# A written order for the first phases of an attention and expert kernel, with its scales taken another way

## The chip, the core and the metric

The kernel runs on one core of a Trainium2 chip. The core has a matrix engine (PE), a vector engine (DVE), an activation engine (ACT), a general engine (POOL, GpSimd) and a queue that issues loads and stores (SP). Each takes its own instructions in order and waits for the others by semaphores. The metric is device microseconds (us) of one execution, lower is better. Profiled and timed executions are of the same program on the same inputs.

## The reference

```python
q, k, v: (8, 12, 448, 64) float32     # batch, heads, tokens, head size
w_in: (768, 2048) float64, w_out: (2048, 768) float64
scores = scale * q @ k.T - log(448)   # scale = 1 / sqrt(64)
attn   = 1 / (1 + exp(-scores))       # a sigmoid, not a softmax
x      = (attn @ v), heads side by side: (8 * 448, 768)
h      = x @ w_in
g      = where(h > 0, h, exp(min(h, 0)) - 1)
out    = g @ w_out                    # (3584, 768) float32
```

The weights arrive as float64. The kernel turns them into numbers that its engines can work on with integer instructions on the words.

## The kernel before

**Numbers in two parts.** Most matmuls work on float16 pairs: a float32 tile times a power of two gives a high part (ACT, line 139, a product rounded to float16) and a low part (DVE, line 140, the same product less the high part). A product of two such numbers takes three matmuls (high by high, low by high, high by low). The power of two comes from the greatest magnitude of the tile: a reduction, or a matmul with ones that sums magnitudes over the partitions, then a floor (`max`), the exponent's bits (`bitwise_and`, lines 103 to 107 and 179 to 186) and a reciprocal.

**Weights.** w_in is cut into 16 tiles of 128 columns (768 KB of float64 each), w_out into two halves of 16 tiles (384 KB each). `magnitudes` (line 150) builds a float32 number from the words of a float64: two ACT passes (lines 156 and 160), a DVE pass (161), and a matmul with ones that sums the magnitudes. `signed` (172) puts the sign back with a second DVE pass. Then the tile is split in two (139 and 140). `w_in_tile` does all of it for w_in and leaves the result in `wi`; `load_w_out` is a generator that does it for w_out, one step at a time.

**Buffers.** `stage` (line 195) holds five float64 tiles of w_in and five float32 tiles. It carries the tag "wo", which is also that of `wo` (line 693), w_out's own tile; both lie in one buffer, one after the other. `g`, the hidden layer, has a tag that it shares with `early`, the float32 keys and queries of batch 0. PSUM has three buffers of tag "pm", two of "psc" and one of "pav".

**Stages.** For each of 8 batches there are 6 pairs of heads. Batch 0 (EXACT = 1) computes its attention in float32: `transposed` turns q and k on PE (line 362), `scores` (408), a sigmoid on ACT (416), `values` (480 and 468), `finish` (`xh`, high and low part and its greatest magnitude). From batch 1 on, q and k are split first ("nat", then a transposing DMA to "qk"), and from the ninth pair on the values too. When six pairs are done, `rescale` brings the six parts of `xh` to one scale (521), `greatest` finds its power of two, and `moe1` computes 16 tiles of the hidden layer: 18 matmuls each (570), an exponential (582), two DVE passes (584 and 585) and the split into `g`. `moe2` multiplies `g` by w_out (602) and writes the result (610 and 612).

**Order.** For the first part, up to batch 0's hidden layer, a planner with a time model orders the instructions of each engine. The loop there takes pair after pair of batch 0 with some tiles of w_in behind each (`W_IN`), and `w_out_beside` puts w_out's steps beside batch 0's hidden layer. From line 779 on, the order of PE, ACT, DVE and SP is that of the program text: the attention of batch b runs beside `moe2` of batch b - 1, whose steps `fill` hands out between scores and values. The rest of w_out's steps stand at the first pairs of batch 1 (`step`, line 825). `beside` prepares two pairs of the next batch during `moe1`. POOL is left to the planner throughout. Sigmoids of a batch are made to follow the last exponential of the batch before (`last_exp`), so that the activation tables change once each way.

**Scales.** `value_scale` keeps, pair after pair, the greatest value scale (`vm`) and its reciprocal (`vi`) on DVE. `moe_scales` makes the 16 factors of the exponential (`m[:, 0]`) and of the split (`m[:, 1]`) in three DVE instructions.

Of the kernel before, what the change touches and what calls it, by code (L numbers as in the profile page):

```python
# [32 lines left out]

@with_exitstack
def attention_ffn(
# [24 lines left out]
    WHOLE = EXACT * NP + 2  # L60
    SP = 4
    SKEW = 2
    W_IN = [1, 3, 6, 9, 12, 15, 16]
    W_LOAD = [1, 1]
    W_OUT = 4
    W_AHEAD = [6, 2]
# [12 lines left out]
    wi = const.tile([P, 2, NK, DF], F16, name="wi")  # L79


    wp = const.tile([P, NF], F32, name="wp")
    wr = const.tile([P, NF], F32, name="wr")
# [6 lines left out]
    stage, w_in_words = [], []  # L90
    ones = const.tile([P, P], BF16, name="ones")
    nc.vector.memset(ones, 1.0)
    half = const.tile([P, 2], BF16, name="half")
# [14 lines left out]

    def greatest(dst, mx):
# [4 lines left out]
        def rest():  # L114
            pb = ps.tile([P, 512], F32, tag="pm", name="pb", bufs=3)
            nc.tensor.matmul(pb[:, :P], ones, dg, start=True, stop=True)
            al = sb.tile([P, 1], F32, tag="al", name="al", bufs=2)
            nc.vector.tensor_reduce(al, pb[:, :P], axis=AX.X, op=ALU.max)
            power_of_two(dst, al, XTINY)

        return rest

    def sums_of_rows(dst, mx, parts):

        n = mx.shape[1]

        def rest():
            pb = ps.tile([P, 512], F32, tag="pm", name="pr", bufs=3)
            sums = pb[:, : 4 * n].rearrange("p (n x) -> p n x", x=4)
            for r in parts:  # L130
                nc.tensor.matmul(sums[r], ones[:, r], mx, start=True, stop=True)
            al = sb.tile([P, n], F32, tag="al", name="al", bufs=2)
            nc.vector.tensor_reduce(al, sums, axis=AX.X, op=ALU.max)
            power_of_two(dst, al, TINY)

        return rest

    def split(hi, lo, src, s):
        nc.scalar.mul(hi, src, s)  # L139
        nc.vector.scalar_tensor_tensor(lo, src, s, hi, op0=ALU.mult, op1=ALU.subtract)  # L140
# [9 lines left out]
    def magnitudes(t, lo, hi, hl, sums, start, stop):  # L150


        u, h = t.bitcast(U32), hi.bitcast(F32)


        nc.scalar.activation(t, h, AF.Abs, scale=2.0**-112)


        top = hl.bitcast(U16).rearrange("p a (c t) -> p a c t", t=4)[:, :, :, 1]
        nc.scalar.activation(lo, top, AF.Copy, scale=2.0**-13, bias=2.0**-14 - 0.5)  # L160
        nc.vector.scalar_tensor_tensor(
            u, u, 3, lo, op0=ALU.logical_shift_left, op1=ALU.bitwise_or
        )

        top = t.bitcast(BF16).rearrange("p a (c t) -> p a c t", t=2)[:, :, :, 1]
        n = t.shape[1]
        for c in range(n):
            nc.tensor.matmul(
                sums, ones, top[:, c], start=start and c == 0, stop=stop and c == n - 1
            )  # L170
# [17 lines left out]
    def load_w_in(n):  # L188

        src = w_in.rearrange("(c p) f -> p c f", p=P)  # L190
        for _ in range(n):
            f = len(w_in_words)
            if f == 0:

                stage.append(sb.tile([P, WR * 2 + WT, NK * P], F32, tag="wo", name="stage"))
            if f < NF:
                st = stage[0][:, f % WR * 2 : f % WR * 2 + 2]
                st = st.rearrange("p a c -> p (a c)").rearrange("p (c x) -> p c x", c=NK)
                nc.sync.dma_start(st.bitcast(U64), src[:, :, f * P : (f + 1) * P])
                w_in_words.append(words(st))  # L200

    def w_in_tile(f):
        lo, hi, hl = w_in_words[f]
        t = stage[0][:, WR * 2 + f % WT].rearrange("p (c x) -> p c x", c=NK)
        sums = ps.tile([P, 512], F32, tag="pm", name=f"si{f}", bufs=3)
        magnitudes(t, lo, hi, hl, sums[:, :P], True, True)
        sum_magnitude(wp[:, f : f + 1], sums[:, :P])
        nc.vector.reciprocal(wr[:, f : f + 1], wp[:, f : f + 1])
        s = sb.tile([P, 1], F32, tag="sw", name=f"swi{f}", bufs=2)
        nc.gpsimd.tensor_scalar(s, wr[:, f : f + 1], 2.0**WTOP, None, op0=ALU.mult)  # L210
        d = wi[:, :, :, f * P : (f + 1) * P]
        signed(t, hi)
        split(d[:, 0], d[:, 1], t, s)
# [6 lines left out]
    def load_w_out(wo):  # L220


        for i in range(NH):
            whole = [
                wo[:, i, f + SKEW].rearrange("p j c -> p (j c)").bitcast(F32)
                for f in range(NF - SKEW)
            ] + [
                sb.tile([P, HM], F32, tag="o", name=f"to{i}_{f}", bufs=OB) for f in range(SKEW)
            ]
            sums = ps.tile([P, 512], F32, tag="pav", name=f"so{i}")  # L230
            loads = []

            def load(f):
                if f >= NF:
                    return
                if i == 0 and f >= 2:
                    st = wo[:, 1, f % 8 * 2 :][:, :2]
# [12 lines left out]
                loads.append(st)  # L250

            early = W_AHEAD[i]
            for f in range(early):
                load(f)
            for f in range(NF):
                load(f + early)
                lo, hi, hl = words(loads[f])
                t = whole[f].unsqueeze(1)
                magnitudes(t, lo, hi, hl, sums[:, :HM], f == 0, f == NF - 1)
                signed(t, hi)  # L260
                yield
            sum_magnitude(wop[:, i : i + 1], sums[:, :HM])
# [3 lines left out]
            for f in range(NF):  # L266
                split(wo[:, i, f, 0], wo[:, i, f, 1], whole[f], s[:, 1 + f : 2 + f])
                yield


    last_exp = {}
# [3 lines left out]
    def load_qk(b, hp):  # L275
# [3 lines left out]
        for i, src in enumerate((q, k)):  # L279
            for j in range(2):  # L280
                nc.sync.dma_start(  # L281
                    raw[:, i * (NC + 1) :][:, :NC, j],
                    src[b, h0 + j, :SM].rearrange("(p c) d -> p c d", c=NC),
                )
# [19 lines left out]
    def value_scale(b, hp, pv, c, xs):  # L304
# [3 lines left out]
        if hp:  # L308
            nc.vector.tensor_tensor(vm[:, hp : hp + 1], vm[:, hp - 1 : hp], pv, op=ALU.max)
        else:  # L310
            nc.gpsimd.tensor_copy(vm[:, 0:1], pv)
        nc.vector.reciprocal(vi[:, hp : hp + 1], vm[:, hp : hp + 1])
        if b * NP + hp < WHOLE:
            nc.gpsimd.tensor_scalar(c, vi[:, hp : hp + 1], 2.0 ** (XTOP - XBITS), None, op0=ALU.mult)
        else:
            nc.gpsimd.tensor_scalar(
                c, vi[:, hp : hp + 1], pv, 2.0 ** (XTOP - XBITS - TOP - ATOP),
# [3 lines left out]
    def prepare(b, hp, raw, rv, xs):  # L321


        u = f"{b}_{hp}"
        n = 1 if b < EXACT else 3
        mx = sb.tile([P, 15], BF16, tag="mx", name=f"mx{u}", bufs=2)
        groups = mx.rearrange("p (n x) -> p n x", x=5)[:, :n, :4]
        absmax(mx[:, 0:4], rv.rearrange("p (a t) d -> p a (t d)", a=4))
        if n > 1:

            absmax(mx[:, 6 : 2 * NC + 7], raw.rearrange("p t h d -> p t (h d)"))
            nc.vector.tensor_tensor(
                mx[:, 5:14:8], mx[:, 9:10].to_broadcast([P, 2]), half, op=ALU.mult
            )
        pw = sb.tile([P, n], F32, tag="pw", name=f"pw{u}", bufs=2)
        apart = b >= EXACT and (hp > 2 or hp == (2 if b == EXACT else 0))
        product = sums_of_rows(pw, groups, rows if apart else [slice(0, P)])

        def scales():
            product()  # L340
            sc = sb.tile([P, n + 3], F32, tag="sc", name=f"sc{u}", bufs=5)
            if b >= EXACT:
                nc.vector.reciprocal(sc[:, :n], pw)
                nc.gpsimd.tensor_scalar(sc[:, :n], sc[:, :n], 2.0**TOP, None, op0=ALU.mult)

                for i, r in enumerate(rows):
# [3 lines left out]
                    sc[:, n + 2 :], pw[:, 1:2], pw[:, 2:3], 2.0 ** (-2 * TOP) / math.sqrt(D),  # L350
                    op0=ALU.mult, op1=ALU.mult,
                )
            value_scale(b, hp, pw[:, 0:1], sc[:, n : n + 1], xs)
            return lambda: transposed(sc)

        def transposed(sc):
            x_scale, s_rest, s_scale = (sc[:, n + i : n + i + 1] for i in range(3))
            if b < EXACT:
                pt = ps.tile([P, 2, 512], F32, tag="psc", name=f"pt{u}", bufs=2)
                pt = pt.rearrange("p a x -> p (a x)")  # L360
                for t in range(2 * NC + 1):
                    nc.tensor.transpose(
                        pt[:, t * P : (t + 1) * P], raw[:, t].rearrange("p h d -> p (h d)"), ident
                    )
                qk = early[:, hp % 2]
                nc.vector.tensor_copy(qk, pt[:, : 2 * S])
                return x_scale, 1 / math.sqrt(D), [qk], [rv]
# [502 lines left out]
```

## Time and profile before

| what | us |
|---|---|
| median of three runs | 1201.78 |
| the three runs | 1201.60 to 1202.27 |
| the profiled execution, its own time | 1201.61 |
| its span on the core | 1199.8 |

The span is the time from the first to the last instruction that the profile shows; about 1.8 us lie around it. In the profile's rows L570 is line 570 of the kernel, "x16" a count of instructions, "mean ns" the length of one, and behind the bar stands the time that the engine sat idle before them and who released it. PEld is the loading of weights on PE, SPq the load queue. PEclk is the clock that PE was granted, in tenths of the full one in the slices and as a share in the windows. A window's row gives its length, then the busy time of each engine in it with the count of instructions, the clock, the mean share of the 16 DMA engines, and the GB/s that they moved.

### The profile page before, as it was taken

The numbers are of one execution on the slowest core, as the hardware profiler recorded it, in microseconds if no ns is written. First come the engines' busy times: TensorE is split into PE (matmuls) and PEld (weight loads), VectorE is DVE, ScalarE is ACT, GpSimd is POOL, SyncE is SP. The second block draws the span as 40 slices with busy tenths as digits, with TensorE's granted clock in tenths as the row PEclk, the third lists the DMA queues.
The fourth block names the chain that finished last, engine by engine and source line by source line (L and its number), as shares of the span: only waits on it lengthen the run. The fifth ranks groups of instructions, "written<-read, shape, count | busy, mean of one in ns | idle before, by whom it ended". The sixth has DMA issues, their size and how long they took to land.

```text
span 1199.8 us, 24004 instructions
## 1 busy us (share of the span) xinstructions
PE 1148.5 (96%) x9662; PEld 634.7 (53%) x9662; DVE 817.2 (68%) x1730; ACT 710.1 (59%) x1087; POOL 95.9 (8%) x275
## 2 busy tenths in 40 slices
PE   6779976999999999999999999999999999999998
PEld 2224433555566555555566555655566555655565
DVE  4798888877577575876677575976667666864500
ACT  4785796855566447864666446865666446864300
POOL 1011001100011001100011000200011000100000
PEclk9989988999999999999999999999999999999999
DMA  8874634521234130531224221441134212310000
GB/s 220 260 191 96 220 107 114 104 61 41 47 79 95 34 68 20 115 78 40 41 65 96 53 51 37 94 100 40 40 61 93 61 40 47 70 30 8 1 27 27
DMA packets 220687, 92.14 MB, mean 77 GB/s; under 512 B 184224, under 2 KB 216480, under 8 KB 220576
## 3 DMA queue, kind: packets, MB, share of 16 engines
q1 hardware_dynamic: 220576, 90.61, 31.3%
q8 instruction: 75, 1.23, 0.4%
q14 instruction: 36, 0.29, 0.1%
HBM read 60.29 MB, written 11.01 MB: 59 GB/s over the span
## 4 chain that ended last, share of the span: by engine, by line
PE 85%; DMA 5%; DVE 4%; ACT 3%; SPq 2%; issue 1%; DVEq 0%; POOL 0%; ACTq 0%; POOLq 0%
PE ph L570 32%; PE po L602 31%; PE pav L480 7%; PE psc L408 7%; PE po_r L602 5%; DMA stage<-in_moe_w_in_dram 3%; PE pscr L500 1%; DMA wo<-in_moe_w_out_dram 1%; SPq L281 1%; ACT sg L416 1%; DMA so<-in_moe_w_out_dram 1%; ACT wo L139 1%; DVE wo L175 1%; DVE wo L140 1%; DVE wi L140 1%
## 5 line engine op out<-in xcount | busy, mean ns | idle before, releaser
L570 PE MATMUL ph<-xh,wi 128*128 128x448 f16 x2304 | 441.7, 353 | 1.7 <-DVE e L585 0.9
L602 PE MATMUL po<-wo,g 128*64 128x384 f16 (+1 forms) x4320 | 395.7, 328 | 6.9 <-ACT wo L139 3.8
L602 PEld LDWEIGHTS <-g 128*64 128x64 f16 (+1 forms) x4992 | 290.3, 109 | 169.6 <-issue 40.4
L570 PEld LDWEIGHTS <-wi 128*128 128x128 f16 x2304 | 223.0, 98 | 214.3 <-issue 8.0
L582 ACT ACTIVATE e<-ph,msc 128x448 f32<-128x448 f32 x128 | 80.7, 631 | 185.8 <-PE ph L570 161.1
L455 DVE SCALAR_TENSOR_TENSOR at<-sg,at 128x896 f16<-128x896 f32 x120 | 127.6, 1091 | 92.2 <-ACT at L454 92.2
L416 ACT ACTIVATE sg<-psc,bias,sc 128x896 f32<-128x896 f32 x126 | 133.5, 1094 | 3.6
L584 DVE TENSOR_SCALAR e<-e 128x448 f32<-128x448 f32 x128 | 50.2, 393 | 117.1 <-ACT e L582 117.1
L454 ACT ACTIVATE at<-sg 128x896 f16<-128x896 f32 x120 | 109.4, 947 | 0.6
L139 ACT ACTIVATE g<-e,msc 128x384 f16<-128x384 f32 (+1 forms) x192 | 96.1, 533 | 11.3 <-DVE e L585 9.9
L139 ACT ACTIVATE xh<-pav,sc 128x448 f16<-128x448 f32 x48 | 30.3, 631 | 119.8 <-PE pav L480 117.3
L140 DVE SCALAR_TENSOR_TENSOR g<-e,msc,g 128x384 f16<-128x384 f32 (+1 forms) x192 | 94.8, 522 | 1.9 <-ACT g L139 1.5
L585 DVE SCALAR_TENSOR_TENSOR e<-ph,msc,e 128x448 f32<-128x448 f32 x128 | 87.5, 684 | 4.1
L408 PE MATMUL psc<-qk 64*128 64x448 f16 x756 | 86.5, 352 | 2.2 <-ACT sg L416 2.2
L480 PE MATMUL pav<-at,vn 128*64 128x448 f16 x720 | 74.8, 353 | 0.0
L139 ACT ACTIVATE nat<-raw,sc 128x384 f16<-128x384 f32 (+1 forms) x126 | 60.7, 535 | 10.2 <-POOL sc L347 8.4
L480 PEld LDWEIGHTS <-vn 128*64 128x64 f16 x880 | 49.9, 110 | 31.2
L349 POOL TENSOR_SCALAR sc<-pw 128x1 f32<-128x1 f32 x42 | 12.2, 292 | 662.7 <-DVE pw L105 563.8
L602 PE MATMUL po_r<-wo,g 128*64 128x384 f16 (+1 forms) x672 | 64.9, 327 | 0.0
L140 DVE SCALAR_TENSOR_TENSOR nat<-raw,sc,nat 128x384 f16<-128x384 f32 (+1 forms) x126 | 60.6, 526 | 3.9 <-ACT nat L139 1.8
L140 DVE SCALAR_TENSOR_TENSOR xh<-pav,sc,xh 128x448 f16<-128x448 f32 x48 | 32.6, 680 | 37.1 <-ACT xh L139 37.1
L610 DVE TENSOR_SCALAR o<-po,osc 128x384 f32<-128x384 f32 x48 | 29.4, 612 | 41.1 <-PE po L602 36.4
(112 smaller groups left out, 928.5 us busy)
## 6 DMA issues: line engine op xcount, KB each, us to landing
stage<-in_moe_w_in_dram SPq DMA_DIRECT2D x16, 768.0 KB, 6.6
raw<-in_q_dram SPq DMA_DIRECT2D x96, 96.0 KB, 3.3
raw<-in_k_dram SPq DMA_DIRECT2D x96, 96.0 KB, 2.9
rv<-in_v_dram SPq DMA_DIRECT2D x48, 192.0 KB, 2.8
out_dram<-o SPq DMA_DIRECT2D x48, 192.0 KB, 2.1
wo<-in_moe_w_out_dram SPq DMA_DIRECT2D x19, 384.0 KB, 3.8
so<-in_moe_w_out_dram SPq DMA_DIRECT2D x13, 384.0 KB, 3.7
rv<-in_v_dram SPq DMA_DIRECT2D x96, 32.0 KB, 2.5
```

The costliest lines, as they stand in the source:

```text
L139: nc.scalar.mul(hi, src, s)
L140: nc.vector.scalar_tensor_tensor(lo, src, s, hi, op0=ALU.mult, op1=ALU.subtract)
L408: nc.tensor.matmul(psc[:, j, :S] if g < NC else psc[rows[j], 0, :S], kk[rows[j], o], qq[rows[j], :S], start=(n == 0), stop=(n == len(parts ...
L416: a = nc.scalar.activation(to, psc, AF.Sigmoid, bias=bias, scale=self.s_scale)
L454: nc.scalar.mul(hi, sg, 2.0**ATOP)
L455: nc.vector.scalar_tensor_tensor(lo, sg, 2.0**ATOP, hi, op0=ALU.mult, op1=ALU.subtract)
L480: nc.tensor.matmul(pav[rows[j], :S], vv[i][:, 2 * NC + j if g == NC else j * NC + g], sg[k][:, j], start=(g == 0 and n == 0), stop=(g == N ...
L570: nc.tensor.matmul(ph[:, :S], wi[:, wj, c, f * P : (f + 1) * P], xh[:, c, xj], start=(n == 0), stop=(n == 3 * NK - 1),)
L582: a = nc.scalar.activation(e, ph[:, :S], AF.Exp, scale=inv)
L584: nc.vector.tensor_scalar(e, e, 1.0, -1.0, op0=ALU.min, op1=ALU.add)
L585: nc.vector.scalar_tensor_tensor(e, ph[:, :S], inv, e, op0=ALU.mult, op1=ALU.max)
L602: nc.tensor.matmul(po[r, :HM], tokens[:, r], wo[:, i, f, wj], start=(n == 0), stop=(n == 3 * NF - 1),)
```

## The change

**The order.** The planner's part and the first batch of the written part are replaced by a string, ORDER, of 973 letters. Each letter is a stream, a generator; the program takes the next step of the stream that the letter names. So the order of every engine, now POOL too, is that of the string, from the first load to the rescaling of batch 1. Behind it the old loop goes on from batch 1's hidden layer, with the same shares of `fill`.

```diff
+ORDER = (
+    "iiqviiqviAAAABCDEiBadbCFGcDeSEAABSCFGEiAABDCaDETTFSbSWTATAdWWWqviiFAXAAAGceBCSGEDBYYSCEa"
...
+    streams = {
+        "q": qk_loads(), "v": v_loads(), "i": load_w_in(), "o": load_w_out(),
+        "t": pair_turned(), "u": whole_values(), "j": outputs(),
+        "A": w_in_fields(), "B": w_in_magnitudes(), "C": w_in_add(), "D": w_in_scales(),
+        "E": w_in_signs(), "F": w_in_high(), "G": w_in_low(),
+        "H": w_out_fields(), "I": w_out_magnitudes(), "J": w_out_add(), "K": w_out_signs(),
+        "L": w_out_scales(), "M": w_out_high(), "N": w_out_low(),
+        "a": maxima(), "b": maxima_sums(), "c": pair_scales(), "d": pair_transposes(),
+        "e": pair_copies(), "f": pair_high(), "g": pair_low(),
+        "S": scores(), "T": sigmoids(), "U": sigmoids_high(), "V": sigmoids_low(),
+        "W": value_products(), "X": x_high(), "Y": x_low(),
+        "s": first_scales(), "n": w_in_ratios(),
+        "R": rescaled(), "r": greatest_product(),
+        "m": first_layer("products"), "x": first_layer("exponential"),
+        "y": first_layer("elu"), "z": first_layer("high"), "w": first_layer("low"),
+        "p": output_products(), "k": evictions(),
+    }
...
-    with tc.manual_schedule(engines={E.PE, E.Activation, E.DVE, E.SP}):
+    with tc.manual_schedule(engines={E.PE, E.Activation, E.DVE, E.Pool, E.SP}):
+        for c in ORDER:
+            next(streams[c])
```

The `last_exp` dependency goes. By the string, all 24 sigmoids of batch 0 come ahead of the first of the 16 exponentials, and the rest behind the last one.

**Buffers.** `wo` and `g` are tiles of their own from the start. The float64 tiles of w_in lie in the second half of `wo` and in a part of `g`; its five float32 tiles lie in the first plane of `g`, in rows that the hidden layer writes later.

```diff
+    wo = const.tile([P, NH, NF, 2, HM], F16, name="wo")
+    g = const.tile([P, 2, NF, SM + 2 * R], F16, name="g")
+    stage = g[:, 0, 1:].rearrange("p f s -> p (f s)").bitcast(F32)
...
+    doubles = [
+        wo[:, 1, 4 * r : 4 * r + 4].rearrange("p f j c -> p (f j c)") for r in range(WR - 1)
+    ] + [g[:, 1, :6].rearrange("p f s -> p (f s)")]
+    early = g[:, 1, NF - 7 :].rearrange("p f s -> p (f s)").bitcast(F32)
```

**Scales.** Twice the inverse of a power of two comes from the complement of its exponent's bits, in one DVE instruction; the floor becomes a ceiling of the inverse (or a floor of the power) on POOL. For w_in only the inverse is made; the matmul with ones uses ones that carry the factor.

```diff
+    def twice_inverse(dst, x, least):
+        nc.vector.tensor_scalar(
+            dst.bitcast(U32), x.bitcast(U32), EXPONENT, EXPONENT,
+            op0=ALU.bitwise_and, op1=ALU.bitwise_xor,
+        )
+        nc.gpsimd.tensor_scalar(dst, dst, 2 / least, None, op0=ALU.min)
...
+            nc.vector.tensor_reduce(m, w_in_sums.pop(f)[:, :P], axis=AX.X, op=ALU.max)
+            twice_inverse(ws[:, f : f + 1], m, TINY * 2.0 ** (1 - WTOP))
...
-            nc.vector.tensor_tensor(vm[:, hp : hp + 1], vm[:, hp - 1 : hp], pv, op=ALU.max)
+            nc.gpsimd.tensor_scalar(vm[:, hp : hp + 1], vm[:, hp - 1 : hp], pv, None, op0=ALU.max)
+            nc.gpsimd.tensor_scalar(vi[:, hp : hp + 1], vi[:, hp - 1 : hp], iv, None, op0=ALU.min)
...
-        nc.vector.reciprocal(vi[:, hp : hp + 1], vm[:, hp : hp + 1])
```

The two columns of `mx` that serve both heads' remaining rows (line 332) are made on POOL too. The layer's scales move to POOL, and for batch 0 they are made in four groups of four tiles each (stream `s`):

```diff
+    def moe_scales(m, xs, xr, f=slice(0, NF)):
+        nc.gpsimd.tensor_scalar(
+            m[:, 0, f], wp[:, f], vm, 2.0 ** (XBITS - XTOP - 1 + TOP - 1),
+            op0=ALU.mult, op1=ALU.mult,
+        )
+        nc.gpsimd.tensor_scalar(m[:, 1, f], ws[:, f], vi, xr, op0=ALU.mult, op1=ALU.mult)
...
+    def first_scales():
+        for n in range(4):
+            f = slice(n * NF // 4, (n + 1) * NF // 4)
+            nc.vector.tensor_scalar(
+                wp[:, f].bitcast(U32), ws[:, f].bitcast(U32), EXPONENT, None,
+                op0=ALU.bitwise_xor,
+            )
+            moe_scales(*layer_scales, f)
+            yield
```

**Loads.** The loads of q and of k take both heads of a pair at once, one DMA each where there were two.

```diff
-            for j in range(2):
-                nc.sync.dma_start(
-                    raw[:, i * (NC + 1) :][:, :NC, j],
-                    src[b, h0 + j, :SM].rearrange("(p c) d -> p c d", c=NC),
-                )
+            nc.sync.dma_start(
+                raw[:, i * (NC + 1) :][:, :NC],
+                src[b, h0 : h0 + 2, :SM].rearrange("h (p c) d -> p c h d", c=NC),
+            )
```

The rest of the diff cuts the old functions into the steps that the streams need: `prepare` becomes the class `Preparation`, `moe1` the class `Expert`, `split` a high and a low step. Which pairs are exact, how many matmuls a product takes and in what order a product's matmuls stand stays. `K`, a count of pairs of batch 1 that would be exact too, is 0.

More of the change, by code (lines that the diff above doesn't have):

```diff
@@ L168, in magnitudes @@
             nc.tensor.matmul(
[L169 removed]
+                sums, by, top[:, c], start=start and c == 0, stop=stop and c == n - 1
             )
@@ L202, in w_in_tile @@
[L202 to L213, printed above, removed]
+        for f in range(NF):
+            st = doubles[DOUBLE[f]].bitcast(U64).rearrange("p (c x) -> p c x", c=NK)
+            nc.sync.dma_start(st, src[:, :, f * P : (f + 1) * P])
+            w_in_words.append(words(st))
+            yield
@@ L218, in w_in_ratios, with load_w_out @@
         nc.gpsimd.tensor_scalar(wn, wp, wm[:, 1:2], 2.0**WTOP, op0=ALU.mult, op1=ALU.mult)
-    def load_w_out(wo):
+        yield
+    w_out_words, w_out_whole, w_out_sums, w_out_scale = {}, {}, {}, {}
+    def load_w_out():
         for i in range(NH):
[L224 to L237, printed above, removed]
+            for f in range(NF):
+                if i == 0 and f >= AB:
+                    st = wo[:, 1, (f + 4 - AB) % 8 * 2 :][:, :2]
                 elif i == 1 and f % 2 and f < NF - SP - SKEW:
@@ L333, in prepare, with sums @@
                 mx[:, 5:14:8], mx[:, 9:10].to_broadcast([P, 2]), half, op=ALU.mult
             )
[L335 to L344, printed above, removed]
+        def sums(self):
+            b, hp = self.b, self.hp
+            apart = not self.exact and (hp > 2 or hp == (2 if b == EXACT else 0))
+            groups = self.mx.rearrange("p (n x) -> p n x", x=5)[:, : self.groups, :4]
+            self.reach = sums_of_rows(groups, rows if apart else [slice(0, P)])
@@ L346, in scales @@
+        def scales(self):
+            n = self.groups
+            pw = sb.tile([P, n], F32, tag="pw", name=f"pw{self.u}", bufs=2)
+            sc = sb.tile([P, n + 3], F32, tag="sc", name=f"sc{self.u}", bufs=5)
+            self.reach(pw, sc[:, :n])
+            if not self.exact:
                 for i, r in enumerate(rows):
@@ L707, in hidden @@
-    def hidden(b, beside=None):
-        xh, xs = xh_of.pop(b), xs_of.pop(b)
-        whole = rescale(b, xh, xs)
-        next(whole)
-        yield
-        xp, xr, rest = next(whole)
-        m = sb.tile([P, 2, NF], F32, tag="msc", name=f"msc{b}")
-        def first():
-            rest()
-            moe_scales(m, xs, xr)
-        moe1(b, g, xh, m, first, beside)
-        yield b, xs, xp
+    begun, of_pair, preparation = {}, {}, {}
+    later = []
+    def pair_of(n):
+        if n not in of_pair:
+            b, hp = pairs[n]
+            if hp == 0:
+                xh_of[b] = []
+                if b == EXACT and K:
+                    ahead = sb.tile([P, K, 2, S], F16, tag="xa", name="xa")
+                    xh_of[b] += [ahead[:, c] for c in range(K)]
+            if len(xh_of[b]) == hp:
+                here = sb.tile([P, NK, 2, S], F16, tag="xh", name=f"xh{b}")
+                xh_of[b] += [here[:, c] for c in range(hp, NK)]
+            of_pair[n] = Pair(b, hp, *ready.pop(n), xh_of[b], xs_of[b])
+        return of_pair[n]
@@ new lines, in qk_loads, with v_loads, maxima, maxima_sums @@
+    def qk_loads():
+        for n in range(AHEAD + 2):
+            raws[n] = load_qk(*pairs[n])
+            yield
+    def v_loads():
+        for n in range(AHEAD + 2):
+            loaded[n] = raws.pop(n), load_v(*pairs[n])
+            yield
+    def maxima():
+        for n in range(AHEAD + 1):
+            p = begin(n)
+            p.greatest()
+            yield
+            if not p.exact:
+                p.greatest_qk()
+                yield
+    def maxima_sums():
+        for n in range(AHEAD):
+            preparation[n].sums()
+            yield
@@ new lines, in x_high, with x_low, layer, first @@
+    def x_high():
+        for n in range(LAST):
+            of_pair[n].finish_high()
+            yield
+    def x_low():
+        for n in range(LAST):
+            of_pair[n].finish_low()
+            yield
+            of_pair[n].finish_most()
+            yield
+    def layer(b):
+        xh, xs = xh_of.pop(b), xs_of.pop(b)
+        whole = rescale(b, xh, xs)
+        for _ in range(NP + 1):
+            next(whole)
+            yield
+        next(whole)
+        yield
+        xp, xr, last = next(whole)
+        m = sb.tile([P, 2, NF], F32, tag="msc", name=f"msc{b}")
+        def first():
+            reciprocal = last()
+            def rest():
+                reciprocal()
+                nc.gpsimd.tensor_scalar(
+                    xr, xr, 2.0 ** (XTOP - XBITS + GTOP - 2 - WTOP - TOP), None, op0=ALU.mult
+                )
+                if b:
+                    moe_scales(m, xs, xr)
+                else:
+                    layer_scales.extend([m, xs, xr])
+            return rest
+        yield Expert(b, xh, m), first, (b, xs, xp)
```

740 lines of the change are left out of this document (470 added, 270 removed).

## The prediction

> **What bounds the kernel now.** I read the engine table and the slices first, then the windows between four events on PE, then PE's waits, then the groups.
>
> ```profile
> PE 1148.5 (96%) x9662; PEld 634.7 (53%) x9662; DVE 817.2 (68%) x1730; ACT 710.1 (59%) x1087; POOL 95.9 (8%) x275
> PE   6779976999999999999999999999999999999998
> DVE  4798888877577575876677575976667666864500
> PEclk9989988999999999999999999999999999999999
> core 0: us, PE busy (x) PEld busy (x) DVE busy (x) ACT busy (x) POOL busy (x), PEclk, DMA share, GB/s
> 0.00:95.78 95.78, 68.27 (x355) 27.12 (x356) 70.49 (x173) 63.59 (x81) 8.48 (x28) 0.95 0.79 213
> 95.78:156.24 60.46, 57.21 (x306) 28.66 (x304) 52.47 (x130) 41.46 (x80) 5.46 (x17) 1.00 0.53 159
> 156.24:199.76 43.52, 27.16 (x208) 12.08 (x209) 37.56 (x81) 36.31 (x65) 4.73 (x11) 0.84 0.43 120
> 199.76:257.06 57.30, 57.30 (x646) 33.60 (x646) 47.72 (x95) 44.03 (x62) 6.67 (x21) 1.00 0.46 100
> sum 257.06, PE 209.94 PEld 101.45 DVE 208.23 ACT 185.39 POOL 25.33; mean PE 52.49 PEld 25.36 DVE 52.06 ACT 46.35 POOL 6.33
> ```
>
> PE is the bound over the whole span, but not at its start. The four stretches end with batch 0's first expert tile (95.78), its first output product (156.24), the last gap on PE (199.76) and batch 1's first expert tile (257.06). Inside the 257.06 us PE is idle for 257.06 - 209.94 = 47.1 us: 27.5 in the first stretch, 3.3 in the second, 16.4 in the third, none in the fourth. The granted clock is 0.95 and 0.84 where the idle is, and 1.00 elsewhere. Behind 257.06 the slices show PE at nine tenths or more until the last one.
>
> ```profile
> 1078.50:1199.80 121.30, 117.08 (x675) 65.62 (x673) 36.28 (x83) 23.48 (x49) 0.62 (x2) 0.99 0.05 15
> PE pav L480 <- ACT sg L416: 5.6, 4, 2.2
> PE pav L480 <- DVE xh L140: 5.3, 1, 5.3
> 6.74 5.51 DMA stage<-in_moe_w_in_dram
> PE so L168 <- DVE wo L161: 4.6, 3, 4.0
> PE po L602 <- ACT wo L139: 3.8, 2, 3.6
> DVE stage L161 <- ACT stage L160: 8.5, 5, 4.3
>   DMA stage<-in_moe_w_in_dram: 16.4, 5
> ```
>
> The last stretch has 4.2 us without PE: the last eviction and its transfer, which the change leaves. The next rows are of the chain of waits (start, length), of PE's and DVE's waits (total, times, longest) and of what idles around w_in's staging. PE's waits name ACT and DVE: sigmoids, the xh split, and in the third stretch w_out's integer work and its split. Behind these stand, in the last two rows, DVE waiting for ACT and the engines waiting for w_in from DRAM (16.4 us). So the first phases are held by the chain load, ACT, DVE, with DVE at 70.49 of 95.78 and 37.56 of 43.52 us.
>
> **The change part by part.** The matmuls stay, but for the order in which they are issued. Everything from batch 0 to batch 1's expert layer now follows the string ORDER on every engine, POOL and the load queue too. I count letters on both sides of the first `p` (an output product of batch 0).
>
> What is behind the first `p` on PE: 96 `p` of 6 matmuls, 16 score steps and 3 of the shared last keys, the value products of six pairs.
>
> ```profile
> 213.11 5.00 PE po L602 x60
> 220.19 1.24 PE psc L408 x12
> 236.76 0.69 PE pscr L500 x12
> 230.18 2.08 PE pav L480 x22
> 188.16 3.90 PE L480 MATMUL pav<-sg,vw 128*64 128x448 f32 x12 [1.12 <-DVE alw L182]
> ```
>
> A `p` is 5.00/10 = 0.50 us, so 48.0 in all; scores 16 x 0.62 + 3 x 0.69 = 12.0; four float16 pairs 4 x 2.08 = 8.3; two float32 pairs at about 3.9 each, 7.8; three `J` and four small sums 0.9. Together 77 us, and in the old order such a mixture ran without a gap (the fourth stretch).
>
> What DVE must do before: the third tile row of `g` and the sixteenth `N` (w_out's first half split) stand just ahead of the first `p`. DVE's work up to batch 1's layer is 208.23. From this I take what lies behind the first `p`:
>
> ```profile
> L140 DVE SCALAR_TENSOR_TENSOR wo<-wo,swo 128x384 f16<-128x384 f32 x28 | 16.6, 613 | 1.6 <-ACT wo L139 1.0
> L455 DVE SCALAR_TENSOR_TENSOR at<-sg,at 128x896 f16<-128x896 f32 x12 | 12.8, 1092 | 6.2 <-ACT at L454 6.2
> 7.37 1.23 SPq L281 DMA_DIRECT2D raw<-in_q_dram  x2
> L140 DVE SCALAR_TENSOR_TENSOR xh<-pav,sc,xh 128x448 f16<-128x448 f32 x12 | 8.1, 675 | 0.7 <-ACT xh L139 0.7
> L143 DVE TENSOR_REDUCE xs<-xh 128x1 f32<-128x448 f16 x12 | 7.3, 609 | 0.0
> L143 DVE TENSOR_REDUCE mx<-raw 128x7 bf16<-128x896 f32 x8 | 8.6, 1079 | 0.0
> 136.80 0.56 DVE L161 SCALAR_TENSOR_TENSOR wo<-wo 128x384 uint32<-128x384 uint32 x1
> 137.27 0.40 DVE L584 TENSOR_SCALAR e<-e 128x448 f32<-128x448 f32 x1
> L183 DVE TENSOR_SCALAR alw<-alw 128x1 f32<-128x1 f32 x18 | 2.5, 147 | 0.0
> ```
>
> 16 `N`, 6 `k`, 16 `g` and 5 `I`/`K` are 43 at about 0.61 = 26.2; `V` 12 x 1.09 and 8 of half height, taken at 0.62, = 18.1; `Y` 6 x (0.68 + 0.61) = 7.7; `a` 4 x 1.08 and 4 at about 0.68 = 7.0; the rescale and some 15 small ones about 4.5. That is 63.5 us in 103 instructions. A queued DVE instruction starts 0.47 us behind one of 0.56 (rows 136.80 and 137.27), so each occupies 0.08 less than its length: 63.5 - 8.2 = 55.3.
>
> The guards: per w_in tile three DVE instructions (the floor, the mask, the reciprocal) become one, per pair about five become two, in all some 65 fewer. Each is 0.15 us long (row L183), at least 0.07 when queued: 4.5 to 10 us, I take 7. DVE work ahead of the first `p`: 208.2 - 7 - 55.3 = **146 us**. PE has 209.9 - 77 = 133 us there at the clock it was granted, fewer at full clock; ACT, by the same count, about 126. So DVE binds this part, though not by much.
>
> **The sum.** DVE can begin at about 8 us: w_in's first load is now the first issue at 0.7, takes 5.5 us (row 6.74) and then two ACT passes of 0.9. Before, it began this work at 14.0 (first start in the row of L161 further down). If it is busy for a share e from there, its last piece, needed by the sixteenth `p`, ends at 8 + 146/e; the first `p` starts 16 x 0.50 = 8 us earlier, and 77 us follow: batch 1's layer starts at **77 + 146/e**. The break-even against 257.06 is e = 0.81. The rows give e = 0.80 for the first stretch (70.49 over 87.8 from 8 us on), 0.87 for the second and 0.86 for the third. Why more now: before, w_out's tile and w_in's staging shared one buffer, so w_out's loads began behind w_in's last split, and
>
> ```profile
> 90.00:120.00 30.00, 27.50 (x158) 13.91 (x155) 26.77 (x78) 15.19 (x25) 4.94 (x15) 1.00 0.43 96
> 130.00:177.00 47.00, 39.58 (x251) 19.28 (x251) 43.83 (x96) 39.95 (x77) 3.32 (x8) 0.93 0.40 130
> 30.00:60.00 30.00, 21.59 (x120) 8.18 (x122) 22.80 (x54) 23.25 (x31) 1.88 (x6) 0.97 0.90 260
> ```
>
> the DMA share falls to 0.43 at 90 to 120 us. Now w_out has a tile of its own, w_in's float32 tiles lie in `g`, and 11 of the 32 `o` loads, 22 `H` and 7 `I` stand ahead of the first expert tile `m`, while three `F` and five `G` of w_in move behind it. Where loads keep up DVE reached 43.83/47 = 0.93 (130 to 177). I take 0.87 for the 72 us ahead of `m`, between 0.80 and 0.93, and 0.93 for the 74 behind: 82.8 + 79.6 = 162.4, e = 0.90. End: 77 + 162 = 239, against 257.06 a gain of 18. The profiled execution took 1201.61 (span 1199.8), 0.17 under the median, which I neglect: **1184 us**. Bounds of e: 1.00 gives an end of 223 and 1167.5; 0.81 gives nothing.
>
> Parts without a term. Merging q's and k's two loads per pair into one saves two issues per pair on the load queue, each 0.62 us (row 7.37); the same 256-byte pieces move. It is inside e; eight pairs stand ahead of `m`, so 0 to -10 us, near 0 where the queue waits for buffers or bandwidth anyway. The order has all exponentials between the two blocks of sigmoids, so the activation tables change as often as before. Behind 257.06 DVE's savings are worth nothing, since PE has no gap. The layer scales, now POOL's, stand ahead of each batch's first exponential:
>
> ```profile
> 261.74 1.28 ACT L582 ACT_TABLE_LOAD   x1 [5.96 <-DVE msc L539]
> 264.13 0.68 DVE L585 SCALAR_TENSOR_TENSOR e<-ph,msc,e 128x448 f32<-128x448 f32 x1
> L628 POOL TENSOR_SCALAR osc<-osc,xs,rr 128x2 f32<-128x2 f32 x7 | 2.9, 414 | 127.3 <-DVE rr L105 127.3
> L210 POOL TENSOR_SCALAR swi<-wr x16: 205/208/1042, 24.2 to 99.4; 128x1 f32<-128x1 f32 x16
> L161 DVE SCALAR_TENSOR_TENSOR stage<-stage x16: 936/950/959, 14.0 to 87.4; 128x768 uint32<-128x768 uint32 x16
> ```
>
> Two POOL instructions at about 0.41 come ahead of the table load at 261.74; behind it on ACT stand the exponentials, and PE needs the first tile's PSUM buffer again only at the fifth tile, some 6 us after it comes free at 264.8. Cost 0; without that cover 0.8 x 7 batches = 6 us.
>
> The last two rows also bear on the guards' new engine: POOL's scale takes 0.21 us at best and 1.04 at worst, DVE's pass beside it 0.94 to 0.96. So POOL waits for DVE here, and DVE shows no stretch. The Trainium skill (SBUF — State Buffer, section "SBUF: two separate sides") says that the two share a port pair as an exclusive lock: a DVE instruction with two SBUF inputs and a GpSimd one block each other for a whole instruction. The row agrees for POOL's side; no run here shows the other side.
>
> **The rivals.** *Denser* (e of 0.94 or more): the search has hidden nearly every wait, end at 223 to 232, 1167.5 to 1177. For it: ACT and PE have 20 us of slack ahead of `p`. Against: DMA. *Loads hold the front*: ahead of `m` stand 13 to 16 w_in tiles of 0.79 MB, 11 halves of 0.39 MB and 8 pairs of 0.69 MB, 22.4 MB; at 260 GB/s (row 30:60) 86 us, at the first stretch's 213 GB/s 105. In the second case 105 + 74/0.93 - 8 + 77 = 254: 1198; with all in between, 1191 to 1199.4. *DVE blocked by POOL*: some 47 more POOL instructions ahead of `p`, each holding DVE for 0.2 us, 9 us: 1193. The rule of the Trainium skill's SBUF page would give this one. *No change*: end within 2.4 us of 257. *Slower*: engines that take work in a fixed order stand behind a late load with ready work queued behind them; before, the planner could pass it. Place: `A` and `B` on w_in, `H` and `I` on w_out. There are 48 such loads; it decides from 18/48 = 0.38 us of uncovered wait each over my e; at 0.5 us the end is 239 + 24 = 263, 1207. The row of 16.4 us in 5 waits for w_in shows that single waits of 3 us occur.
>
> **How the numbers follow.** Forecast (e 0.86 to 0.94, 1177 to 1191) 0.48; denser 0.17; loads hold 0.12; blocked by POOL 0.04; no change 0.08; slower 0.11. Faster by over 0.2% (about what a measurement of this kernel can tell) is 0.48 + 0.17 + 0.12 + 0.04 = 0.81. The range of 1168 to 1200 leaves out a little of the densest case and nearly all of the slower one.
>
> **What would show it.** In the changed profile: batch 1's first expert tile near 239 instead of 257; PE idle before it near 30 us instead of 47, mostly ahead of the first `m`; the first output product near 162, with no gap on PE behind it; DVE busy about 146 us by 170; DMA share above 0.43 at 90 to 120 us; the rest from batch 1's layer to the end 942.7 us as before. Wrong, if gaps appear behind the first output product, if PE waits in steady state for POOL's scales, or if DVE waits for w_in for more than 16 us.

## The result, and the profile after

The changed kernel takes 1172.08 us (median of four, 1171.42 to 1172.90) against 1201.93; the ratio is 0.9752 with a 95% interval of 0.9735 to 0.9769. The forecast was 1184, its range 1168 to 1200. The profiled execution took 1171.42 us with a span of 1169.6. The page of the changed kernel, its engines and slices:

```profile
PE 1141.7 (98%) x9662; PEld 635.5 (54%) x9662; DVE 785.4 (67%) x1506; ACT 705.7 (60%) x1087; POOL 179.6 (15%) x491
PE   5989999999999999999999999999999999999998
DVE  6999988866666667866666666767576575855400
PEclk9999999999999999999999999999999999999999
DMA  9986445311242113512044121622134131310000
```

PE has as many matmuls as before. It is now busy for nine tenths or more from the fourth slice on, but for the last one, and its granted clock is at nine tenths or more in every slice. The first three windows below are cut where batch 0's first expert tile starts on PE (85.28), where its first output product starts (148.26) and where batch 1's first expert tile starts (226.78). The fourth row is the three together. The last two go from 8 us, where the prediction let DVE begin (its first pass on w_in starts at 7.09), to the sixteenth step of the output products (156.46).

```profile
0.00:85.28 85.28, 64.85 (x346) 26.18 (x347) 70.62 (x143) 68.46 (x93) 21.23 (x63) 0.96 0.96 266
85.28:148.26 62.98, 60.97 (x327) 30.76 (x327) 62.00 (x135) 49.13 (x95) 16.47 (x29) 1.00 0.54 156
148.26:226.78 78.52, 77.26 (x840) 45.40 (x839) 70.02 (x129) 66.48 (x100) 18.62 (x43) 1.00 0.49 103
0.00:226.78 226.78, 203.07 (x1510) 102.34 (x1510) 202.64 (x405) 184.07 (x286) 56.31 (x135) 0.98 0.68 179
8.00:85.28 77.28, 64.85 (x346) 26.07 (x346) 69.42 (x139) 65.02 (x89) 20.23 (x54) 0.96 0.98 269
85.28:156.46 71.18, 68.92 (x421) 37.24 (x420) 70.13 (x150) 56.66 (x108) 16.47 (x29) 1.00 0.51 148
```

One of the cuts of before is not the same event. Batch 0's first expert tile starts there at 91.26; 95.78 is the end of its last two matmuls:

```profile
91.26 3.19 PE L570 MATMUL ph<-xh,wi 128*128 128x448 f16 x16
95.24 0.54 PE L570 MATMUL ph<-xh,wi 128*128 128x448 f16 x2 [0.79 <-DVE xh L140]
```

From start to start, the part ahead of the first expert tile takes 85.3 us instead of 91.3, the part from there to the first output product 63.0 instead of 65.0, and the part from there to batch 1's layer 78.5 instead of 100.8. Most of the gain shows in the last part, where PE's waits for w_out are gone.

Batch 1's layer starts at 226.78 instead of 257.06, 30.3 us earlier; what follows takes 1169.6 - 226.8 = 942.8 us, as before (942.7). So the whole difference lies in the first phases. PE is idle there for 226.8 - 203.1 = 23.7 us instead of 47.1, and busy for 203.1 instead of 209.9 on the same matmuls, at a clock of 0.98 instead of 0.95. Between the first expert tile and the first output product DVE is busy for 62.0 of 63.0 us and PE for 61.0: both are nearly full. Some of the waits that PE still has:

```profile
PE si L220 <- DVE g L211: 14.0, 7, 8.1
PE psc L549 <- DVE g L490: 1.8, 1, 1.8
PE so L220 <- DVE xh L186: 1.5, 1, 1.5
PE ph L723 <- DVE wi L186: 0.9, 1, 0.9
PE po L785 <- DVE e L740: 0.5, 1, 0.5
```

The 8.1 us in the first row is the start: PE's first instruction is now a sum for w_in, so it begins at 8.1 instead of 4.65. Of PE's 16.4 us of idle time in the third stretch of before, where it waited for w_out's passes and splits above all, little is left: behind the first output product PE is idle for 78.5 - 77.3 = 1.3 us.

### The profile page after: what moved, and what is told of

It is laid out like the page before. It is cut to its first block, busy times and chain, and to the rows that moved or that the text cites. A ratio compares the mean times of both kernels' runs of the same rounds, so it can differ in the third digit from the quotient of the medians.

```text
span 1169.6 us, 23893 instructions
## 1 busy us (share of the span) xinstructions
PE 1141.7 (98%) x9662; PEld 635.5 (54%) x9662; DVE 785.4 (67%) x1506; ACT 705.7 (60%) x1087; POOL 179.6 (15%) x491
## 4 chain that ended last, share of the span: by engine, by line
PE 81%; DVE 3%; ACT 2%; issue 1%; DMA 0%; POOL 0%; DVEq 0%; ACTq 0%; POOLq 0%
PE ph L723 33%; PE po L785 29%; PE pav L619 7%; PE psc L549 6%; PE po_r L785 5%; PE pscr L649 1%; ACT sg L557 1%; DVE wo L186 1%; DVE g L186 1%; DVE at L186 0%; DMA so<-in_moe_w_out_dram 0%; ACT at L587 0%; DVE nat L186 0%; ACT nat L501 0%; DVE mx L193 0%
## 5 line engine op out<-in xcount | busy, mean ns | idle before, releaser
L785 PEld LDWEIGHTS <-g 128*64 128x64 f16 (+1 forms) x4992 | 291.3, 109 | 160.1 <-issue 30.3
L626 ACT ACTIVATE xh<-pav,sc 128x448 f16<-128x448 f32 x48 | 30.3, 632 | 127.7 <-PE pav L619 122.6
L145 POOL TENSOR_SCALAR sc<-sc 128x3 f32<-128x3 f32 (+1 forms) x48 | 11.7, 244 | 432.4 <-DVE pw L178 432.3
```

What stands on the lines that cost most here:

```text
L785: nc.tensor.matmul(po[r, :HM], tokens[:, r], wo[:, i, f, wj], start=(n == 0), stop=(n == 3 * NF - 1),)
```

## The experiments

Each ratio is to the kernel before on the same chip; "slower" and "more" below are against the changed kernel's 1172.1. The kernel before took 1201.7 to 1202.1 on the three chips used, so that times of different chips can be compared. Single times of one kernel spread over 1.5 to 6 us, so differences below 2 us are not told apart.

**1. The planner in the string's place.** The same instructions and buffers; the string is only the program text. Here and in experiment 2 batch 1's sigmoids are again made to follow batch 0's last exponential; these lines are left out below.

```diff
...
-    with tc.manual_schedule(engines={E.PE, E.Activation, E.DVE, E.Pool, E.SP}):
-        for c in ORDER:
-            next(streams[c])
+    for c in ORDER:
+        next(streams[c])
+    with tc.manual_schedule(engines={E.PE, E.Activation, E.DVE, E.Pool, E.SP}):
```

> The same instructions, buffers and scales as the changed kernel, but for the part that the string orders the planner is free to order each engine (the string is only its program text); sigmoids of batch 1 follow the last exponential of batch 0, as before. Theory A (the written order is what keeps DVE and PE full): most of the gain of 29.8 us goes, 1188 to 1202 us. Theory B (the separate buffers, the lighter DVE work and the merged loads are it): within 6 us of the changed kernel, 1172 to 1178 us.

1206.5 us (1205.0 to 1209.1), ratio to before 1.0041 (1.0026 to 1.0056): 4.7 us slower than the kernel before. All of the gain goes. But here the planner also orders what stood in a written order before. Its windows, cut at its first expert tile (88.03), first output product (168.28) and batch 1's layer (260.40):

```profile
0.00:88.03 88.03, 63.26 (x337) 24.86 (x338) 71.56 (x141) 71.45 (x98) 20.20 (x60) 0.95 0.96 265
88.03:168.28 80.25, 67.61 (x335) 32.65 (x333) 69.76 (x155) 50.91 (x99) 18.02 (x37) 0.92 0.54 147
168.28:260.40 92.12, 82.32 (x841) 46.03 (x840) 59.16 (x110) 62.00 (x92) 13.38 (x38) 0.94 0.28 64
```

The front takes 88 us, hardly more than under the string. The stretch behind takes 80 instead of 63, with DVE busy for 69.8 of 80.3 us where the string had 62.0 of 63.0, and from the first output product on, where the written order takes 78.5, it takes 92.

**2. The planner up to the first output product only,** the string behind it.

```diff
...
+    for c in ORDER[: ORDER.index("p")]:
+        next(streams[c])
     with tc.manual_schedule(engines={E.PE, E.Activation, E.DVE, E.Pool, E.SP}):
-        for c in ORDER:
+        for c in ORDER[ORDER.index("p") :]:
             next(streams[c])
```

> As the kernel that leaves the first part to the planner (1206.5 us), but only up to the first output product of batch 0; from there to batch 1's expert layer the written order holds, as a written order held there before the change. If the order ahead of the first output product is what the change gains: that stretch ends near 168 us as under the planner, 78.5 us follow, batch 1's layer starts at 247: 1191 to 1195 us. If the whole loss of the planner's kernel lay behind that point: 1172 to 1180 us.

1189.1 us (1187.8 to 1192.9), ratio 0.9904 (0.9884 to 0.9923). The first output product starts at 165.8 and batch 1's layer at 243.2, 77.4 us later:

```profile
87.27:165.80 78.53, 64.70 (x336) 32.01 (x335) 69.43 (x155) 51.72 (x99) 18.88 (x36) 0.96 0.51 137
165.80:243.16 77.36, 76.76 (x841) 44.22 (x840) 60.49 (x112) 61.98 (x91) 18.10 (x39) 1.00 0.37 88
```

So the order ahead of the first output product is worth 17.0 of the 29.8 us. The other 12.8 come without it: from the scales, the buffers, the loads in the string's text, and the string's own part behind the first output product, which runs here as in the changed kernel. In the kernel before the first output product starts earlier than here (156.2), but 100.8 us follow it; here 77.4 do.

**3. One more DVE pass, and 4. two more matmuls, in each of batch 0's 16 expert tiles.**

```diff
...
+            if self.b == 0:
+                nc.vector.tensor_scalar(pad, pad, 1.0, None, op0=ALU.mult)
...
+            for _ in range(2 if b == 0 else 0):
+                nc.tensor.matmul(
+                    self.ph[f], wi[:, 0, 0, f * P : (f + 1) * P], self.xh[0][:, 0],
+                    start=True, stop=True,
+                )
```

> One more DVE instruction of 128x448 float32 (a pad tile times 1, 0.39 us long, some 0.31 us of the engine) in each of batch 0's 16 expert tiles: 5.0 to 6.2 us of DVE work between the first expert tile and the first output product. If DVE binds that stretch: 4 to 6 us slower. If PE binds it (61.0 of 63.0 us busy): 0 to 2 us. If both are full: 4 to 6 us here and in the kernel with more PE work.

> Two more matmuls of 128x448 at the head of each of batch 0's 16 expert products (their results are overwritten): 32 x 0.19 = 6.0 us of PE work in the same stretch. If PE binds it: 5 to 6 us slower. If DVE alone binds it: 0 to 3 us.

With the DVE passes 1176.1 us (1173.4 to 1176.5), with the matmuls 1174.3 (1172.7 to 1176.4): 4.0 and 2.2 us more. In the profiled executions the stretch from the first expert tile to the first output product grows from 63.0 to 67.2 and to 65.9 us, first with the DVE passes, then with the matmuls:

```profile
85.55:152.73 67.18, 61.72 (x327) 30.75 (x326) 66.19 (x149) 49.60 (x96) 16.78 (x29) 1.00 0.52 146
86.74:152.59 65.85, 65.85 (x359) 33.85 (x359) 63.35 (x136) 49.81 (x97) 14.43 (x29) 1.00 0.53 150
```

DVE binds the stretch: its busy time grows by 4.2 us and the stretch by the same 4.2, with 1.0 us of DVE idle in both kernels. PE is close behind: the 32 matmuls add 4.9 us of busy time, 0.15 each instead of the 0.19 estimated; 2.0 of it fill PE's idle time, which falls to nothing, and the stretch grows by the other 2.9. The two medians, 4.0 and 2.2 us, lie too close together for their spread to tell the engines apart; the windows do. In the profiled run with the matmuls 1.5 us of delay (86.7 against 85.3) stand ahead of the first added matmul and so are not its effect.

**5. The guards back on DVE.**

```diff
-        nc.gpsimd.tensor_scalar(dst, dst, 2 / least, None, op0=ALU.min)
+        nc.vector.tensor_scalar(dst, dst, 2 / least, None, op0=ALU.min)
...
-            nc.gpsimd.tensor_scalar(vm[:, hp : hp + 1], vm[:, hp - 1 : hp], pv, None, op0=ALU.max)
+            nc.vector.tensor_scalar(vm[:, hp : hp + 1], vm[:, hp - 1 : hp], pv, None, op0=ALU.max)
...
```

> The floors and ceilings of the scales, and the running greatest scale of the values, go from POOL back to DVE; all else is the changed kernel (1172.1 us). Theory (DVE is full ahead of the first output product, 62.0 of 63.0 us): some 52 more DVE instructions stand there, each occupying 0.07 to 0.15 us, so 4 to 8 us slower. Rival (the way over POOL costs as much as it saves, since POOL's scale for w_in now takes 0.52 us on average and ACT waits 2.8 us for it): within 1.5 us, or faster.

1177.8 us (1177.5 to 1180.0), ratio 0.9800 (0.9786 to 0.9815): 5.7 us slower. The first expert tile starts at 89.2 instead of 85.3, the first output product at 153.7 instead of 148.3. DVE has 62 more instructions up to batch 1's layer, not 52, and is busy there for 212.0 instead of 202.6 us.

**6. The new scales alone, on the kernel before.** Complement, guards on POOL and POOL's columns of `mx` in the old kernel, its planner, buffers and loads kept.

```diff
-        sum_magnitude(wp[:, f : f + 1], sums[:, :P])
-        nc.vector.reciprocal(wr[:, f : f + 1], wp[:, f : f + 1])
+        m = sb.tile([P, 1], F32, tag="alw", name="alw", bufs=2)
+        nc.vector.tensor_reduce(m, sums[:, :P], axis=AX.X, op=ALU.max)
+        nc.vector.tensor_scalar(
+            wr[:, f : f + 1].bitcast(U32), m.bitcast(U32), EXPONENT, EXPONENT,
+            op0=ALU.bitwise_and, op1=ALU.bitwise_xor,
+        )
...
```

> The kernel before with the new scales alone: complement instead of mask and reciprocal, floors and ceilings, the running scale of the values and the two columns of mx on POOL; planner, buffers, loads and layer scales as before (1201.8 us). Theory (a DVE that is busy for 0.80 to 0.87 of the first phases has room, so lighter work there is worth little): 1198 to 1202 us. Rival (the 5.7 us that the guards cost in the written order are theirs anywhere): 1195 to 1197 us.

1197.2 us (1195.5 to 1198.1), ratio 0.9952 (0.9936 to 0.9969): 4.9 us less. My theory that lighter DVE work is worth little where DVE has room falls: only the slowest single time reaches its range, and the median lies 0.2 us outside the rival's. About 5 us stand in both kernels, though not for the same change: here it is the complement and the guards together, in experiment 5 the guards' engine alone. So a DVE that is idle for a tenth or a fifth of the time can still have its work on the path; which of its instructions were on it was not traced.

**7. Half of w_in's bytes.** Each w_in load brings the first half of its rows, so the result is another. Five memsets on DVE set the other half to zero before the first loads are used.

```diff
+    for st in doubles:
+        nc.vector.memset(st.bitcast(F32)[:, NK * P :], 0.0)
...
-            nc.sync.dma_start(st, src[:, :, f * P : (f + 1) * P])
+            nc.sync.dma_start(st[:, : NK // 2], src[:, : NK // 2, f * P : (f + 1) * P])
```

> Each of the 16 w_in loads brings only the first half of its rows (384 KB instead of 768); the other half of the float64 tile is left at what was there (zeros, or old words), so the result is another. 6.3 MB less at 266 GB/s is 23.6 us of the DMA engines ahead of the first expert tile. If loads bind that part (DMA share 0.96 there): the first expert tile starts at 74 to 80 us instead of 85.3, where DVE's and PE's 65 to 71 us of work bind; 1162 to 1168 us. If DVE, ACT or PE with the fixed order bind it already: 84 to 86 us, 1170 to 1173 us.

1171.0 us (1170.3 to 1172.0); the first expert tile starts at 84.5 instead of 85.3. The windows of this kernel's front, and then the changed kernel's:

```profile
0.00:30.00 30.00, 17.75 (x86) 8.32 (x87) 22.50 (x44) 19.23 (x24) 5.37 (x24) 0.94 0.66 163
30.00:60.00 30.00, 26.74 (x162) 10.62 (x160) 29.04 (x55) 28.97 (x37) 8.52 (x22) 1.00 0.72 189
```

```profile
0.00:30.00 30.00, 17.10 (x82) 7.98 (x84) 18.20 (x36) 18.41 (x23) 5.17 (x23) 0.94 0.94 253
30.00:60.00 30.00, 26.76 (x162) 10.62 (x158) 29.00 (x58) 29.01 (x37) 7.88 (x18) 1.00 1.01 271
```

The DMA share falls from 1.01 to 0.72 at 30 to 60 us, and DVE (29.0) and ACT (29.0 of 30.0) stay as full as they were. In the first 30 us DVE's extra 4.3 us are 3.5 of memsets, which end at 5.2, ahead of its first pass on w_in, and the earlier start of that pass. PE's first matmul starts at 7.1 instead of 8.1, since the first load lands earlier: this accounts for the whole 0.8 us. Behind the start a DMA share near one did not bind.

**8. w_out behind the first expert tile.** In the string w_out's letters ahead of the first `m` are spread evenly between it and the first `p`, and w_in's last parts move ahead of it.

The string around the first `m`, in the changed kernel and in this experiment:

```diff
-    ..."oXTHHTCYYaEaSWWWTWbHHHXHHHHFHooHHFHRIIRcDHfffqvYYJJJJJJIJRRrmKKKKKIKRIsI"...
+    ..."WWTWbXFFRRcDfffqvYYRRrFFFGGGGGmooRHsHIsoosHHgHxHHyHImIIzoxoomooxHaHHgHHy"...
```

> The string with w_out's letters (loads, ACT and DVE passes, sums, splits) that stand ahead of the first expert tile moved behind it and spread evenly up to the first output product, and the three high and five low parts of w_in that stand behind it moved ahead: the division of the stages before the change, in the written order. Theory (pulling w_out forward fills ACT and DVE beside the loads): the first expert tile comes 0 to 6 us earlier, since 4.3 MB less stand ahead of it, the stretch behind takes 75 to 85 us instead of 63; 1178 to 1190 us. If where w_out stands does not matter: 1172 to 1175 us.

1190.0 us (1189.1 to 1190.7), ratio 0.9900 (0.9885 to 0.9915): 17.9 us slower. The first expert tile comes at 82.0, 3.3 us earlier; the stretch behind it takes 84.0 us instead of 63.0. It is an even spreading, not a searched one, so part of the loss may be the spreading.

**9. The first pair's loads first.**

```diff
-    "iiqviiqviAAAA...
+    "qviiiqviiAAAA...
```

> Only the first letters of the string are changed: the first pair's q, k and v are loaded ahead of the first three w_in tiles, as before the change. DVE's first w_in pass stands ahead of the first pair's work on DVE, and the pair's 0.69 MB take 2.7 us at 253 GB/s: if DVE's early start is worth its full length, 3 to 5 us slower (and more where PE's first matmul, a sum for w_in, waits); if later slack takes it up: within 1.5 us.

1176.7 us (1173.2 to 1177.3), 4.6 us slower. PE begins at 13.2 instead of 8.1, and batch 1's layer at 231.9 instead of 226.8: the delay of the start goes through to the end.

**10. One load per head for q and k.**

```diff
-            nc.sync.dma_start(
-                raw[:, i * (NC + 1) :][:, :NC],
+            for j in range(2):
+                nc.sync.dma_start(
+                    raw[:, i * (NC + 1) :][:, :NC, j],
...
```

> q and k of a pair are loaded with one DMA per head again, four instead of two of the larger loads for each pair. Estimate from the rows of before: two issues of 0.62 us for each of 8 pairs, 10 us of the load queue ahead of the first expert tile. If the issues bind there: 5 to 10 us slower. If bandwidth does (DMA share 0.96): within 2 us.

1172.8 us (1171.9 to 1174.5): no difference that can be told. The merged loads are worth nothing that can be measured here. As half of w_in's bytes did not help either, bandwidth is not the likely reason; that the loads run ahead of their use fits, but was not tested by itself.

**11. The layer scales in one group.**

```diff
-            f = slice(n * NF // 4, (n + 1) * NF // 4)
+            if n:
+                yield
+                continue
+            f = slice(0, NF)
```

> Batch 0's 16 layer scales in one group at the place of the first of the four. Theory (off the path; POOL's two instructions take the place of eight): within 1 us of 1172.1. Rival (the first exponential waits for a longer POOL instruction, or all scales must wait for w_in's last tile): 2 to 4 us slower.

1171.7 us (1171.3 to 1173.0): no difference.

**12. A DVE pass moved to POOL.** An attempt at a faster version: the first DVE pass on batch 0's exponentials on POOL.

```diff
-            nc.vector.tensor_scalar(e, e, 1.0, -1.0, op0=ALU.min, op1=ALU.add)
+            first = nc.gpsimd if self.b == 0 else nc.vector
+            first.tensor_scalar(e, e, 1.0, -1.0, op0=ALU.min, op1=ALU.add)
```

> In batch 0's 16 expert tiles the first of the two DVE passes on the exponential (128x448 float32, 0.39 us long) goes to POOL: DVE has 5 us less to do between the first expert tile and the first output product, PE as much as now. PE is busy for 61.0 of those 63.0 us, so at most 2 us are to be had: 1170 to 1172 us. If POOL blocks DVE, or takes much longer for it than DVE: 1174 to 1185 us.

1187.4 us (1183.1 to 1189.0), 15.3 us slower. The view by line, with the least, median and greatest length in ns, and the longest waits (total, times, longest) between 80 and 165 us:

```profile
L740 POOL TENSOR_SCALAR e<-e x16: 1700/1737/3212, 93.5 to 163.2; 128x448 f32<-128x448 f32 x16
L186 DVE SCALAR_TENSOR_TENSOR wo<-wo,swo x13: 599/609/904, 117.5 to 163.0; 128x384 f16<-128x384 f32 x13
L186 DVE SCALAR_TENSOR_TENSOR g<-e,msc,g x11: 671/677/976, 129.1 to 163.5; 128x448 f16<-128x448 f32 x11
DVE e L741 <- POOL e L740: 17.7, 9, 3.9
```

POOL takes 1.7 to 3.2 us for what DVE does in 0.39, and DVE waits 17.7 us for it. No other version that was run is faster than the changed kernel by more than the spread.

## Why the prediction was right, and where its size was off

**The place and the mechanism held.** The gain lies ahead of batch 1's layer, DVE sets the pace ahead of the first output product, and it is the fixed order that fills it. The likeliest case was forecast as an end at 232 to 246; 226.8 lies in the denser rival's 223 to 232. PE is idle for 23.7 us ahead of batch 1's layer (near 30 was forecast), 20.4 of them ahead of the first expert tile; there is no gap worth the name behind the first output product (1.3 us), and in the steady state PE waits for no scale of POOL's. So the way to the result was the one forecast; but the likeliest case was 12 us too slow, by two terms that erred the same way (below). The prediction took 95.78 for the start of batch 0's first expert tile, where it is the end; its e of 0.80 holds for the window as cut.

**77 us behind the first output product:** 78.5 measured, and 77.4 in experiment 2. PE lost 1.3 us there.

**146 us of DVE work ahead:** mis-sized, at 139.5 (69.42 + 70.13 from 8 us to the sixteenth step). The guards saved 208.2 - 202.6 = 5.6 us instead of 7, so the error is on the other side: I counted all that stands ahead of the letter `p` in the string, but the output products wait only for the last `w`, and four `g`, two `K`, two `a` and an `I` stand between the two. In the trace these nine letters' DVE work runs from 156.3, just behind the last `w`, to 161.4: 5.1 us. Another 1.2 us of DVE's work ran ahead of 8 us, and about 1.5 us were counted too little behind the first `p`; the smaller saving takes 1.4 back. At e = 0.90 the 6.5 us are worth 7.2.

**e = 0.90:** the other mis-sized term. It was 139.5/148.5 = 0.94, from 69.42/77.28 = 0.90 in the front (I took 0.87) and 70.13/71.18 = 0.985 behind (I took 0.93). 0.93 was the planner's best over 47 us of the kernel before; the string left 1 us of idle in 71. This is worth 155.0 - 148.4 = 6.6 us. Together they move the first output product from 146/0.90 = 162 to 139.5/0.94 = 148.4 (measured 148.3), and the end, with 78.5 behind it, from 239 to 226.8.

**Loads.** The rival of loads that hold the front came near in rate (266 GB/s against the 260 of its first case, 85.3 us against 86), but experiment 7 shows that this was chance: with 6.3 MB less the front is 0.8 us shorter, and that much by the first load alone. What 22.4 MB would take was computed rightly; that they are waited for was not shown by the share.

**POOL.** That the guards run on POOL is worth 5.7 us (experiment 5), and DVE was not blocked by it:

```profile
L227 DVE SCALAR_TENSOR_TENSOR g<-wo,g x14: 948/950/983, 9.3 to 77.4; 128x768 uint32<-128x768 uint32 x14
L145 POOL TENSOR_SCALAR ws<-ws 128x1 f32<-128x1 f32 x16 | 8.3, 521 | 45.2 <-DVE ws L141 41.1 <-DVE al L175 3.9
```

DVE's pass keeps its 0.95 us, at most 0.98, while POOL's short instruction rose from 0.30 to 0.52 us on average. Experiment 12 does show DVE's side: with POOL instructions of 2 us beside them, splits that take 0.61 and 0.68 us take up to 0.90 and 0.98. By the lock that the Trainium skill describes (SBUF — State Buffer, "SBUF: two separate sides"), a DVE instruction with two inputs in SBUF and a GpSimd instruction that reads SBUF shut each other out: the one that starts first holds the shared ports for its whole length. This case agrees for POOL's side: a scale that takes 0.21 us at best took up to 1.04, and POOL's pass in experiment 12, 1.70 us at best, up to 3.21. For DVE's side it does not: three of DVE's splits lie inside that POOL pass of 3.21 us (from 152.1), and the most that a split was stretched is 0.3 us.

**Steady state.** The cost of 0 for the layer scales on POOL held, by more than its cover. The timeline of the changed kernel at batch 1's layer (start, length):

```profile
230.42 1.28 ACT L733 ACT_TABLE_LOAD   x1 [4.37 <-PE pb L154]
231.60 0.28 POOL L697 TENSOR_SCALAR msc<-wp,xs 128x16 f32<-128x16 f32 x1
231.91 0.63 ACT L733 ACTIVATE e<-ph,msc 128x448 f32<-128x448 f32 x1 [0.21 <-POOL msc L697]
```

The table load no longer stands behind the scale but beside the chain that makes it: before it started behind DVE's scale, now behind PE's small sum. The exponential comes 5.1 us behind the layer's first matmul (226.8), before 6.0 (257.0).

**What gave the 29.8 us:** 17.0 come from the written order ahead of the first output product (experiment 2). In the other 12.8 the scales have about 5 (4.9 alone on the kernel before; in the written order the guards on POOL alone are worth 5.7). The rest, about 8, is a difference and not a measurement: the buffers of their own, the order of the loads and the string's part behind the first output product lie in it, and no run takes them apart. Nor are the shares independent. By experiment 8 a written order that leaves w_out behind the first expert tile is 17.9 us slower; the pulling forward of w_out needs the buffer of its own. The merged loads and the four groups gave nothing that can be measured.

## What to carry to other kernels

Where several engines are nearly full in one stretch, sum each engine's work up to the point that releases the next stretch, divide by the share that an order can reach, and count only what that point truly waits for, not what stands ahead of it in the text. Between the first expert tile and the first output product the written order kept DVE busy for 0.98 of the time, where the planner reached 0.87 and 0.88 with the same instructions in the kernel (experiments 1 and 2). The order up to there was worth more than all the rest of the change together. With the planner over the whole stretch the kernel was even slower than the old one (1206.5 against 1201.8), in spite of its buffers and lighter instructions; the written order behind the first output product alone took 17.4 of the 34.4 us back. A DMA share near one was no proof of a bound here: halve the bytes and see.

## What the runs showed that was not expected

POOL needed 1.7 to 3.2 us for a pass over 128x448 float32 in SBUF that DVE does in 0.39 us, though its scales of one column take 0.21 us at best. And an ACT table load moved ahead by itself: the profile names PE's small sum as its releaser instead of DVE's scale, and it starts 1.2 us ahead of POOL's scale (230.42 against 231.60); why, no run here shows.
